# First units of a linear attention before two MLPs: products in another buffer, weight steps and key copies in another order, eight idle matmuls, later sums

## The chip, the cores and the metric

The kernel runs on one core of a Trainium2 chip as one program. The metric is the device time of one execution in microseconds (us); lower is better. The kernel before takes 982.43 us, the median of three runs (981.87 to 982.62).

## The reference

Inputs are r, k, v, w of shape (4, 8, 768, 48) (batch, heads, time, channel), u of shape (8, 48), and two pairs of MLP weights. All is float32.

```python
for t in range(S):                       # attention with a decaying state
    cur = einsum('bhd,bhe->bhde', u * kt, vt)
    y[:, :, t] = einsum('bhd,bhde->bhe', rt, state + cur)
    state = wt[..., None] * state + einsum('bhd,bhe->bhde', kt, vt)
x = y.transpose(0, 2, 1, 3).reshape(B * S, H * D)      # (3072, 384)
h = x @ moe_w_in;  x = where(h > 0, h, exp(min(h, 0)) - 1) @ moe_w_out
h = x @ moe2_w_in; x = (h / (1 + exp(-h))) @ moe2_w_out
```

Both MLPs have a hidden width of 2048.

## The kernel before

**Units.** The attention is cut into 24 units, one for each chunk of 128 steps and each batch; unit n is chunk n // 4 of batch n % 4. A unit's work has two parts. `prep_steps(n)` makes the decays: `products` (r times k, for the bonus term), `scan` and `scan_back` (the running products of w, forward and backward, in the one tile `both`), `whole_decay`, `far` (an activation over `both` that collects how small the decays get), `q` and `kt` (tiles `tq` and `tk`, scaled by the decays), `summed` (small matmuls of the products with u), and `diag` (copies the sums into `dg` and writes eight scaled identities into the tile `am`). `pe_steps(n)` holds what TensorE does and what goes with it: `scores` (tk by tq), `ktok` (a transpose of tk, tile `ktp`) and `ktok_copy` (ScalarE, into `kt`), `masked` (VectorE copies the scores over `am` above the diagonal), `outer` (kt by v, tile `upd`), `update` (VectorE, the state), `past` and `within` (the output `y`), and `split` (y into two rounded parts `xh`, ScalarE, and `xl`, VectorE).

**Weights.** An MLP's weights come in 16 pieces f0 to f15. A piece is loaded into a staging tile `wst` (three buffers), and `w_scale` (two ScalarE activations, L400 and L402), `w_join` (two VectorE operations, L409 and L411) and `w_split` (`wh` on ScalarE, L423; `wl` on VectorE, L424) make two rounded parts of it. `w_load` issues the loads of the next piece; SyncE's queue stands at that issue until the staging buffer is free.

**Stages.** `dense_units` runs the first four units alone (block 0), each turn of its loop preparing unit n + 1 while unit n is finished. Then the MLP slices begin: for each of six blocks of four units, `slot` runs 16 slices, each a `hidden` (nine matmuls, L438), an activation, and, two slices later, `out_first` (nine matmuls, L469). Between them, ticks bring the next block's units (`round_ticks`; `prep_rest` for the first of them) and, in block 0, the weight pieces. Each slice uses one weight piece. The second MLP follows.

**What sets the order.** Every engine takes its instructions in the order in which the code is written; there is no planner. What an instruction waits for are its operands and the tiles that it overwrites. Tiles of one tag go round a fixed number of buffers: `am` has two, the MLP's `gh` has two, `wst` three.

**Lines.** `products` writes at L215 and L216 into the first half of `am` (`st["af"]`), so for unit n + 1 it needs the buffer that unit n - 1 used, whose last reader is `within` (L356). The dense loop stands at L604 to L656, the ticks at L545 to L586, `prep_rest` at L658.

Of the kernel before, what the change touches and what calls it, by code (L numbers as in the profile page):

```python
# [8 lines left out]
F32 = mybir.dt.float32  # L9
# [11 lines left out]
BLOCKS = (4, 4, 4, 4, 4, 4)  # L21
# [12 lines left out]
def kernel(  # L34
# [21 lines left out]
    nc = tc.nc  # L56
# [3 lines left out]
    RB = w_ch.shape[2]  # L60
    L = 128
    NCH = S // L
    NU = B * NCH
    NP = H // 2
# [6 lines left out]
    g_p = ctx.enter_context(tc.tile_pool(name="g", bufs=2))  # L71
# [30 lines left out]
    ident = const.tile([128, 128], F32, name="ident")  # L102
# [34 lines left out]
    def load_unit(n, names):  # L137
        c, b = divmod(n, B)
        for nm in names if n < NU else "":
            if nm in "rk" and n < SUMMED:  # L140
                continue
            src, shape, pool, bufs = dict(
                w=(w_ch, [RB, W1 + 1], one_p, 2), c=(rk_ch, [RB, 2, NP, L], one_p, 2),
                r=(r_tok, [128, H * D], tok_p, 3), k=(k_tok, [128, H * D], tok_p, 3),
                v=(v_tok, [128, NP, 64 + D], tok_p, 2))[nm]
            t = un[n][nm] = pool.tile(shape, F32, tag="in_rk" if nm in "rk" else f"in_{nm}", name=f"in_{nm}", bufs=bufs)
            nc.sync.dma_start(t, src[b, c])

    def prep_steps(n):

        st = un[n]
# [60 lines left out]
        def products():  # L212
            if n >= SUMMED:
                return
            rk = st["rk"] = st["af"][0:RB, 0:NP * L].rearrange("p (j t) -> p j t", j=NP)  # L215
            nc.vector.tensor_tensor(out=rk, in0=st["c"][:, 0], in1=st["c"][:, 1], op=ALU.mult)  # L216

        def summed(p=None):
# [167 lines left out]
    def w_load():  # L386
        if not halves:
            return
        m, f = halves.pop(0)
        st = stage["st"].tile([128, 2, DM, 2], I32, tag="wst", name="wst")  # L390
        nc.sync.dma_start(st[:, 0].rearrange("p c two -> p (c two)"), (moe_w_in, moe2_w_in)[m].bitcast(I32)[f])
        src = (moe_w_out, moe2_w_out)[m].bitcast(I32)[f * 128:(f + 1) * 128, :]
        nc.sync.dma_start(st[:, 1].rearrange("p c two -> p (c two)"), src)
        loaded.append((m, f, st.rearrange("p o c two -> p (o c) two")))

    def w_scale():
        if loaded:
            m, f, st = loaded.pop(0)
            low, high = st[:, :, 0], st[:, :, 1].bitcast(F32)
            nc.scalar.activation(  # L400
                out=low, in_=low.bitcast(U32), func=ACTF.Copy, scale=(1 - 2.0**-10) * 2.0**-29, bias=-0.4927)
            nc.scalar.activation(out=high, in_=high, func=ACTF.Copy, scale=2.0**-112)  # L402
            scaled.append((m, f, st))

    def w_join():
        if scaled:
            m, f, st = scaled.pop(0)
            low, t = st[:, :, 0], st[:, :, 1]
            nc.vector.scalar_tensor_tensor(  # L409
                out=low, in0=t, scalar=-0x80000000, in1=low, op0=ALU.bitwise_and, op1=ALU.bitwise_or)  # L410
            nc.vector.scalar_tensor_tensor(  # L411
                out=t, in0=t, scalar=3, in1=low, op0=ALU.logical_shift_left, op1=ALU.bitwise_or)
            whole.append((m, f, st[:, :, 1].bitcast(F32)))

    def w_split():
        if whole:
            m, f, t = whole.pop(0)
            h = wpool.tile([128, 2, DM], F32R, tag=f"wh{f}", name=f"wh{f}_{m}")
            l = wpool.tile([128, 2, DM], F32R, tag=f"wl{f}", name=f"wl{f}_{m}")
            for i, nm in enumerate("io"):  # L420
                wh[nm, f], wl[nm, f] = h[:, i], l[:, i]
            h, l = (x.rearrange("p o c -> p (o c)") for x in (h, l))
            nc.scalar.activation(out=h, in_=t, func=ACTF.Copy)  # L423
            nc.vector.tensor_tensor(out=l, in0=t, in1=h.bitcast(F32), op=ALU.subtract)  # L424
# [106 lines left out]
    def round_parts(n, free=None):  # L531

        j = next(j for j in range(len(BLOCKS)) if n < FIRST[j + 1])
        if n == FIRST[j]:
            xts[j] = x_tile(BLOCKS[j] * L)
        pe = pe_steps(n, xts[j], (n - FIRST[j]) * L, free)
        nxt = prep_steps(n + 1) if n + 1 < NU else None

        def do(name, *a):
            if nxt:  # L540
                nxt[name](*a)

        return pe, do

    def round_ticks(n):  # L545
        pe, do = round_parts(n)

        def t0():
            pe["scores"](0)
            do("bonus")  # L550
            do("products")
            do("scan")
            load_unit(n + 2, "kr")

        def t1():
            pe["scores"](1)
            do("summed")
            do("scan_back")
            do("whole_decay")
            load_unit(n + 3, "w")  # L560
            pe["masked"](0)

        def t2():
            pe["masked"](1)
            do("far")
            do("q")
            do("diag")

        def t3():
            pe["ktok"]()  # L570
            pe["ktok_copy"]()
            do("kt")
            do("diag", 1)
            load_unit(n + 3, "c")

        def t4():
            pe["past"]()
            pe["outer"]()
            pe["update"]()

        def t5():
            pe["within"]()
            pe["split"]()
            load_unit(n + 2, "v")

        return [t0, t1, t2, t3, t4, t5]  # L586

    def dense_units():

        count = BLOCKS[0]  # L590
        prep, pe = {}, {}

        banks = [pool.tile([128, NP * L], F32, tag=tag, name="early")
                 for pool, tag, k in ((ps_o, "o", 3), (ps_h, "h", 2)) for _ in range(k)]
        sums_p = banks[2]

        def begin(n):
            pe[n], _ = round_parts(n, [banks[3 * (n % 2)], banks[3 * (n % 2) + 1]])
            pe[n]["scores"](0)
            pe[n]["scores"](1)  # L600
            pe[n]["ktok"]()
            pe[n]["ktok_copy"]()

        for n in range(-1, count):  # L604
            halves_of = iter((0, 1)) if n > 0 else ()

            def part_of_update():
                for e in islice(halves_of, 1):
                    pe[n - 1]["update"]([e])

            more = n + 1 < count
            if more:
                p = prep[n + 1] = prep_steps(n + 1)
                p["bonus"]()
                p["products"]()
                p["scan"]()
            if n == 0:
                prep[n]["diag"](0)
                prep[n]["diag"](1)
            if more:  # L620
                p["summed"](sums_p[:, (n + 1) * H:(n + 2) * H])
                p["scan_back"](part_of_update)
                p["whole_decay"]()
                p["far"]()
                p["q"]()
                p["kt"]()
                load_unit(n + 3, "wc")
            else:
                part_of_update()
                part_of_update()  # L630
            if n >= 0:
                pe[n]["masked"](0)
                pe[n]["masked"](1)
            if n > 0:
                pe[n - 1]["split"]()
            if n >= 0:
                pe[n]["outer"]()
            if more:
                begin(n + 1)
            if n >= 0:  # L640
                w_join()
                pe[n]["past"]()
                pe[n]["within"]()
                load_unit(n + 2, "v")
                if more:
                    p["diag"](0)
                    p["diag"](1)
                w_split()
                w_load()
                w_scale()  # L650
            if n == -1:
                w_start(0)
            if n == KRAT:
                nc.sync.dma_start(u_sb, u.rearrange("h d -> (h d)").unsqueeze(0).to_broadcast([128, H * D]))
        pe[count - 1]["split"]()
        pe[count - 1]["update"]()  # L656

    def prep_rest(at, p):  # L658

        if at == 1:  # L660
            p["bonus"]()
            p["products"]()
            p["scan"]()
            p["summed"]()
            p["scan_back"]()
            p["whole_decay"]()
            load_unit(BLOCKS[0] + 2, "w")
        elif at == 2:
            p["q"]()
            p["kt"]()  # L670
            load_unit(BLOCKS[0] + 2, "c")
            p["far"]()
            p["diag"](0)
            p["diag"](1)
# [302 lines left out]
```

## Time and profile before

| | us |
|---|---|
| median of three runs | 982.43 |
| profiled execution | 982.12 |
| its span | 980.3 |
| TensorE (PE) busy | 944.0 |
| VectorE (DVE) busy | 504.4 |
| ScalarE (ACT) busy | 484.7 |

The span is what the profiler saw of the engines; 1.82 us of the profiled execution lie around it. Busy times are sums over the span: they do not say which engine the others wait for in a given stretch. Times inside the trace count from the span's start. fp32 matmuls leave two records for each instruction. In brackets behind a row stands how long the engine was idle before it and which instruction ended the wait.

### The profile page before, as it was taken

The numbers are of one execution on the slowest core, as the hardware profiler recorded it, in microseconds if no ns is written. First come the engines' busy times: TensorE is split into PE (matmuls) and PEld (weight loads), VectorE is DVE, ScalarE is ACT, GpSimd is POOL, SyncE is SP. The second block draws the span as 40 slices with busy tenths as digits, with TensorE's granted clock in tenths as the row PEclk, the third lists the DMA queues.
The fourth block names the chain that finished last, engine by engine and source line by source line (L and its number), as shares of the span: only waits on it lengthen the run. The fifth ranks groups of instructions, "written<-read, shape, count | busy, mean of one in ns | idle before, by whom it ended". The sixth has DMA issues, their size and how long they took to land.

```text
span 980.3 us, 14115 instructions
## 1 busy us (share of the span) xinstructions
PE 944.0 (96%) x5622; PEld 798.5 (81%) x5622; DVE 504.4 (51%) x782; ACT 484.7 (49%) x841; POOL 134.9 (14%) x101
## 2 busy tenths in 40 slices
PE   6579999999999999999999999999999999999996
PEld 6457777788888877888778889999999999999996
DVE  6779996766766666676447874222212212212111
ACT  4568885454555554555458984333323323323322
POOL 0000003443334344433200000000000000000000
PEclk8659999999999999999999999999999999999998
DMA  8254442221221131220044550010010200200001
GB/s 243 85 166 139 163 147 67 74 80 55 89 62 55 58 103 55 80 87 10 1 145 145 167 188 1 1 65 1 33 33 1 65 1 1 65 1 1 32 1 36
DMA packets 32219, 68.63 MB, mean 70 GB/s; under 512 B 3600, under 2 KB 13968, under 8 KB 32144
## 3 DMA queue, kind: packets, MB, share of 16 engines
q1 hardware_dynamic: 32144, 67.64, 21.7%
q8 instruction: 46, 0.75, 0.3%
q14 instruction: 29, 0.24, 0.1%
HBM read 58.19 MB, written 9.44 MB: 69 GB/s over the span
## 4 chain that ended last, share of the span: by engine, by line
PE 89%; ACT 4%; DVE 3%; issue 1%; DVEq 0%; ACTq 0%
PE ph L438 40%; PE po L477 21%; PE po L469 19%; PE y L336 3%; PE sc L274 2%; PE y L356 2%; ACT am L199 1%; PE ktp L292 1%; PE upd L306 1%; ACT wh L423 1%; DVE wst L411 0%; DVE wst L409 0%; PE early L266 0%; PE sums L223 0%; ACT wst L400 0%
## 5 line engine op out<-in xcount | busy, mean ns | idle before, releaser
L461 DVE TENSOR_TENSOR gl<-g,gh 128x512 fp32r<-128x512 f32 x192 | 140.4, 731 | 312.3 <-ACT gh L460 311.9
L438 PE MATMUL ph<-xh,wh 128*128 128x512 f32 x576 | 230.7, 401 | 3.2 <-ACT xh L368 3.2
L438 PE MATMUL ph<-xl,wh 128*128 128x512 f32 x576 | 228.7, 397 | 0.0
L438 PE MATMUL ph<-xh,wl 128*128 128x512 f32 x576 | 228.0, 396 | 0.0
L460 ACT ACTIVATE gh<-g 128x512 fp32r<-128x512 f32 x192 | 120.8, 629 | 163.7 <-PE po L477 110.1
L438 PEld LDWEIGHTS ph<-xh,wh 128*128 128x128 f32 x576 | 109.6, 190 | 25.7 <-ACT xh L368 3.6
L477 PE MATMUL po<-wh,gl 128*128 128x384 f32 x384 | 129.5, 337 | 0.0
L477 PE MATMUL po<-wh,gh 128*128 128x384 f32 x384 | 129.3, 337 | 0.0
L477 PE MATMUL po<-wl,gh 128*128 128x384 f32 x384 | 129.0, 336 | 0.0
L438 PEld LDWEIGHTS ph<-xh,wl 128*128 128x128 f32 x576 | 109.5, 190 | 23.8
L438 PEld LDWEIGHTS ph<-xl,wh 128*128 128x128 f32 x576 | 109.6, 190 | 19.4 <-DVE xl L369 0.3
L449 ACT ACTIVATE g<-ph 128x512 f32<-128x512 f32 x96 | 57.3, 596 | 137.6 <-PE ph L438 137.5
L469 PE MATMUL po<-gh,wh 128*128 128x512 f32 x288 | 116.3, 404 | 0.0
L469 PE MATMUL po<-gl,wh 128*128 128x512 f32 x288 | 113.0, 392 | 0.0
L469 PE MATMUL po<-gh,wl 128*128 128x512 f32 x288 | 112.8, 392 | 0.0
L445 ACT ACTIVATE g<-ph 128x512 f32<-128x512 f32 x96 | 56.8, 592 | 89.3 <-PE ph L438 89.2
L454 DVE SCALAR_TENSOR_TENSOR g<-g,ph 128x512 f32<-128x512 f32 x96 | 65.5, 682 | 41.5 <-ACT g L447 40.7
L477 PEld LDWEIGHTS po<-wh,gh 128*128 128x128 f32 x384 | 72.2, 188 | 4.3
L477 PEld LDWEIGHTS po<-wl,gh 128*128 128x128 f32 x384 | 72.1, 188 | 4.1
L477 PEld LDWEIGHTS po<-wh,gl 128*128 128x128 f32 x384 | 72.0, 188 | 0.0
L469 PEld LDWEIGHTS po<-gh,wh 128*128 128x128 f32 x288 | 54.3, 189 | 13.0 <-issue 2.3
L227 POOL TENSOR_TENSOR ql<-tq,qh 64x512 fp32r<-64x512 f32 (+1 forms) x30 | 42.3, 1410 | 164.1 <-ACT qh L226 162.9
(88 smaller groups left out, 1108.5 us busy)
## 6 DMA issues: line engine op xcount, KB each, us to landing
wst<-in_moe_w_in_dram SPq DMA_DIRECT2D x32, 384.0 KB, 3.2
wst<-in_moe_w_out_dram SPq DMA_DIRECT2D x32, 384.0 KB, 4.1
in_c<-in_rk_ch_dram SPq DMA_DIRECT2D x24, 448.0 KB, 4.1
in_w<-in_w_ch_dram SPq DMA_DIRECT2D x24, 226.2 KB, 2.7
in_v<-in_v_tok_dram SPq DMA_DIRECT2D x24, 224.0 KB, 2.8
x_d<-x2s SPq DMA_DIRECT2D x18, 256.0 KB, 2.5
xl<-x_d SPq DMA_DIRECT2D x6, 768.0 KB, 5.2
out_dram<-os SPq DMA_DIRECT2D x24, 192.0 KB, 1.9
```

The source lines that it names most:

```text
L227: nc.gpsimd.tensor_tensor(out=lo, in0=x, in1=hi.bitcast(F32), op=ALU.subtract)
L274: nc.tensor.matmul(p[:, jj].rearrange("p e t -> p (e t)"), a[:, j, :], b[:, j].rearrange("p e t -> p (e t)"), start=i == 0, stop=i == len( ...
L336: nc.tensor.matmul(y[p0:p0 + m, kt, :], state[b][:, j, c:c + m], st["q"][:, j, :], start=kt == 0, stop=False, skip_group_check=True)
L356: nc.tensor.matmul(y[32 * base:32 * base + 32, blk // 4, :], vf[:, c:c + 32], st["a"][:, h // 2, h % 2, :], start=not ch and step == 0, st ...
L438: nc.tensor.matmul(ph, lhs, xt[rhs][:, kt, 0:nt], start=n == 0, stop=n == 3 * KT - 1)
L445: nc.scalar.activation(out=g, in_=ph, func=ACTF.Exp)
L449: nc.scalar.activation(out=g, in_=ph, func=ACTF.Silu)
L454: nc.vector.scalar_tensor_tensor(out=g, in0=g, scalar=-1.0, in1=ph, op0=ALU.mult, op1=ALU.max)
L460: nc.scalar.activation(out=gh, in_=g, func=ACTF.Copy)
L461: nc.vector.tensor_tensor(out=gl, in0=g, in1=gh.bitcast(F32), op=ALU.subtract)
L469: nc.tensor.matmul(po[ot][:, 0:nt], lhs, rhs, start=f == 0 and i == 0, stop=f == NF - 1 and i == 2)
L477: nc.tensor.matmul(po[t][:, 0:DM], lhs[:, sl], rhs["o", f], start=f == 0 and i == 0, stop=f == NF - 1 and i == 2)
```

## The change

The products of units 0 to 3 go into a buffer of the tag `gh`, which the MLP's activations use later. In the dense loop, `bonus` (which only takes the `am` buffer for these units) is called after the scans, `outer` and `begin` stand ahead of `masked`, `w_join` stands between `begin` and `masked`, and the key copy and the diagonals of unit n + 1 stand at the end of the turn, behind `w_split` and `w_scale`. After the loop there are eight matmuls of the identity with itself, whose result nobody reads; then `split` of unit 3, then the weight steps that the last turn held before. In the ticks, `summed` moves one tick later.

```diff
         def products():
             if n >= SUMMED:
                 return
-            rk = st["rk"] = st["af"][0:RB, 0:NP * L].rearrange("p (j t) -> p j t", j=NP)
+            if n < BLOCKS[0]:
+                rk = g_p.tile([RB, NP, L], F32, tag="gh", name="rk")
+            else:
+                rk = st["af"][0:RB, 0:NP * L].rearrange("p (j t) -> p j t", j=NP)
+            st["rk"] = rk
             nc.vector.tensor_tensor(out=rk, in0=st["c"][:, 0], in1=st["c"][:, 1], op=ALU.mult)
...
         def t1():
             pe["scores"](1)
-            do("summed")
             do("scan_back")
...
         def t2():
             pe["masked"](1)
+            do("summed")
             do("far")
...
             pe[n]["ktok"]()
-            pe[n]["ktok_copy"]()
+
+        def keep_clock(k):
+            for _ in range(k):
+                nc.tensor.matmul(banks[2][:, 256:384], ident, ident, start=True, stop=True)
 
         for n in range(-1, count):
...
                 p = prep[n + 1] = prep_steps(n + 1)
-                p["bonus"]()
                 p["products"]()
                 p["scan"]()
-            if n == 0:
-                prep[n]["diag"](0)
-                prep[n]["diag"](1)
-            if more:
                 p["summed"](sums_p[:, (n + 1) * H:(n + 2) * H])
                 p["scan_back"](part_of_update)
                 p["whole_decay"]()
+                p["bonus"]()
                 p["far"]()
...
             if n >= 0:
+                pe[n]["outer"]()
+            if more:
+                begin(n + 1)
+                w_join()
+            if n >= 0:
                 pe[n]["masked"](0)
                 pe[n]["masked"](1)
             if n > 0:
                 pe[n - 1]["split"]()
             if n >= 0:
-                pe[n]["outer"]()
-            if more:
-                begin(n + 1)
-            if n >= 0:
-                w_join()
                 pe[n]["past"]()
                 pe[n]["within"]()
                 load_unit(n + 2, "v")
-                if more:
-                    p["diag"](0)
-                    p["diag"](1)
+            if more:
                 w_split()
                 w_load()
-                w_scale()
+                if n >= 0:
+                    w_scale()
+                pe[n + 1]["ktok_copy"]()
+                p["diag"](0)
+                p["diag"](1)
...
+        keep_clock(8)
         pe[count - 1]["split"]()
+        w_join()
+        w_split()
+        w_load()
+        w_scale()
         pe[count - 1]["update"]()
...
             p["scan"]()
-            p["summed"]()
             p["scan_back"]()
...
         elif at == 2:
+            p["summed"]()
             p["q"]()
```

VectorE, the turn that prepares unit 2 and finishes unit 1: from `q` to the next turn's products, before.

```order
L231 TENSOR_TENSOR tq<-in_c,both 112x512
L238 TENSOR_TENSOR tk<-in_c,both 112x512
L283 COPY_PREDICATED am<-upper,early 128x4x128 x2
L369 TENSOR_TENSOR xl<-y,xh 128x3x128
L409 SCALAR_TENSOR_TENSOR wst<-wst 128x768
L411 SCALAR_TENSOR_TENSOR wst<-wst 128x768
L424 TENSOR_TENSOR wl_0_384<-wst,wh_0_383 128x768
L216 TENSOR_TENSOR am<-in_c 112x512
```

The same turn in the changed kernel, whose lines from L219 to L560 are those of before plus four.

```order
L235 TENSOR_TENSOR tq<-in_c,both 112x512
L242 TENSOR_TENSOR tk<-in_c,both 112x512
L413 SCALAR_TENSOR_TENSOR wst<-wst 128x768
L415 SCALAR_TENSOR_TENSOR wst<-wst 128x768
L287 COPY_PREDICATED am<-upper,early 128x4x128 x2
L373 TENSOR_TENSOR xl<-y,xh 128x3x128
L428 TENSOR_TENSOR wl_0_375<-wst,wh_0_374 128x768
L220 TENSOR_TENSOR rk<-in_c 112x512
```

The two joins of piece f0 moved from behind the masks to ahead of them; the products write `rk`.

ScalarE in that turn, before: from unit 2's `far` to the scaling of f1.

```order
L176 ACTIVATE am,sums<-both 112x1031
L368 ACTIVATE xh<-y 128x3x128
L298 ACTIVATE kt<-ktp 128x448
L196 ACTIVATE dg<-early 128x8
L199 ACTIVATE am<-ident,dg 128x128 x8
L423 ACTIVATE wh_0_383<-wst 128x768
L400 ACTIVATE wst<-wst 128x768
L402 ACTIVATE wst<-wst 128x768
```

And in the changed kernel.

```order
L176 ACTIVATE am,sums<-both 112x1031
L372 ACTIVATE xh<-y 128x3x128
L427 ACTIVATE wh_0_374<-wst 128x768
L404 ACTIVATE wst<-wst 128x768
L406 ACTIVATE wst<-wst 128x768
L302 ACTIVATE kt<-ktp 128x448
L196 ACTIVATE dg<-early 128x8
L199 ACTIVATE am<-ident,dg 128x128 x8
```

The weight steps moved ahead of the key copy and the diagonals.

TensorE around the third MLP slice, before: `sc` are the scores of unit 4, the sums are those of unit 5, and `ph` is the slice.

```order
L266 MATMUL sc<-tq,tk 128x128 x8
L223 MATMUL sums<-u_ch,am 128x2 x4
L438 MATMUL ph<-xh,wh_0_521 128x512
L438 MATMUL ph<-xl,wh_0_521 128x512
L438 MATMUL ph<-xh,wl_0_522 128x512
```

In the changed kernel the slice follows the scores at once, and the sums stand behind its last matmul.

```order
L442 MATMUL ph<-xh,wl_0_536 128x512
L227 MATMUL sums<-u_ch,am 128x2 x4
L473 MATMUL po<-gh,wh_0_374 128x512
```

The sums of unit 5 moved behind the nine matmuls of the third slice.

## Rows read from the trace of the kernel before

**Rows 1.** The page's part 1: busy us, share of the span, instructions.
```profile
PE 944.0 (96%) x5622; PEld 798.5 (81%) x5622; DVE 504.4 (51%) x782; ACT 484.7 (49%) x841; POOL 134.9 (14%) x101
```

**Rows 2.** Windows: length, busy us by engine, granted clock, DMA share, GB/s.
```profile
0.00:54.00 54.00, 31.22 (x337) 26.99 (x337) 36.42 (x65) 28.80 (x66) 1.74 (x9) 0.70 0.59 174
...
130.00:980.00 850.00, 842.20 (x4822) 717.38 (x4820) 398.69 (x607) 395.17 (x661) 133.18 (x92) 1.00 0.18 56
```

**Rows 3.** Timeline, VectorE, units 1 and 2: start, us, engine, line, operation.
```profile
15.27 1.36 DVE L283 COPY_PREDICATED am<-upper,early 128x512 f32<-128x512 int8 x2
19.81 0.69 DVE L216 TENSOR_TENSOR am<-in_c 112x512 f32<-112x512 f32 x1 [3.18 <-PE y L356]
...
24.61 0.68 DVE L238 TENSOR_TENSOR tk<-in_c,both 112x512 f32<-112x512 f32 x1
25.33 1.33 DVE L283 COPY_PREDICATED am<-upper,early 128x512 f32<-128x512 int8 x2
...
27.02 0.94 DVE L409 SCALAR_TENSOR_TENSOR wst<-wst 128x768 int32<-128x768 int32 x1
28.00 0.96 DVE L411 SCALAR_TENSOR_TENSOR wst<-wst 128x768 int32<-128x768 int32 x1
32.30 0.96 DVE L424 TENSOR_TENSOR wl<-wst,wh 128x768 fp32r<-128x768 f32 x1 [3.35 <-ACT wh L423]
33.18 0.68 DVE L216 TENSOR_TENSOR am<-in_c 112x512 f32<-112x512 f32 x1
```

**Rows 4.** Timeline, ScalarE, the same turn.
```profile
28.41 0.55 ACT L298 ACTIVATE kt<-ktp 128x448 f32<-128x448 f32 x1 [2.74 <-PE ktp L292]
...
29.05 2.44 ACT L199 ACTIVATE am<-ident,dg 128x128 f32<-128x128 f32 x8
31.40 0.87 ACT L423 ACTIVATE wh<-wst 128x768 fp32r<-128x768 f32 x1
32.17 0.90 ACT L400 ACTIVATE wst<-wst 128x768 int32<-128x768 uint32 x1
...
32.96 0.90 ACT L402 ACTIVATE wst<-wst 128x768 f32<-128x768 f32 x1
```

**Rows 5.** DMA issues at 10.43, 15.33 and 11.29 us: size, us to landing.
```profile
in_c<-in_rk_ch_dram SPq DMA_DIRECT2D x1, 448.0 KB, 4.6
...
in_c<-in_rk_ch_dram SPq DMA_DIRECT2D x1, 448.0 KB, 9.2
...
wst<-in_moe_w_out_dram SPq DMA_DIRECT2D x1, 384.0 KB, 5.9
```

**Rows 6.** Timeline, the last unit of the dense loop and the first slice.
```profile
46.49 0.72 DVE L320 TENSOR_TENSOR state<-upd,whole 48x192 f32<-48x192 f32 x2
...
48.10 2.53 PE L356 MATMUL y<-am,in_v 128*32 128x128 f32 x32 [4.51 <-DVE am L283]
...
53.25 0.51 ACT L368 ACTIVATE xh<-y 128x384 fp32r<-128x384 f32 x1
...
53.82 0.80 PE L438 MATMUL ph<-xh,wh 128*128 128x512 f32 x1 [3.19 <-ACT xh L368]
...
55.02 0.69 DVE L216 TENSOR_TENSOR am<-in_c 112x512 f32<-112x512 f32 x1
```

**Rows 7.** The chain that ended last: start, us, what.
```profile
53.82 4.39 PE ph L438 x9
...
67.82 1.84 PE sums L223 x8
...
130.01 2.27 PE ph L438 x9
```

**Rows 8.** TensorE's waits, 54 to 140 us: total, times, longest.
```profile
PE sums L223 <- DVE seed L156: 4.8, 3, 3.3
```

**Rows 9.** Timeline: the third slice's exponential on ScalarE.
```profile
73.58 0.60 ACT L445 ACTIVATE g<-ph 128x512 f32<-128x512 f32 x1 [1.28 <-PE ph L438]
```

**Rows 10.** Windows over the 16 warm-up matmuls alone: TensorE busy (records).
```profile
1.10:4.90 3.80, 3.80 (x18) 3.80 (x19) 1.00 0.80 225
```

## The prediction

> **What bounds the kernel now.** I read the busy times first, then the stages, the timeline of the dense loop, and the chain that ended last. TensorE is busy for 944.0 of 980.3 us [rows 1], and from 130 us on for 842.20 of 850 us [rows 2]: there it sets the time, and nothing of the change lies there. In the first 54 us it is busy for 31.22 us only [rows 2]. So a microsecond won ahead of the MLP moves all that follows, as long as the slices up to 130 us do not give it back.
>
> In the first 54 us the loop of a turn sets the time. VectorE makes `tk` (ends 24.61 + 0.68 = 25.29), TensorE scores and transposes it, ScalarE copies the keys at 28.41, writes the diagonals until 31.49 and only then `wh` at 31.40 to 32.27 [rows 4]. VectorE meanwhile masks and joins, stands idle for 3.35 us for `wh`, writes `wl` at 32.30 and begins the next unit at 33.18 [rows 3]. A turn is 33.18 - 19.81 = 13.37 us [rows 3]; the next one is 46.49 - 33.18 = 13.31 us [rows 3, 6]. Ahead of that, VectorE waits 3.18 us at 19.81 for `within` of unit 0, because the products overwrite its `am` [rows 3].
>
> **The change part by part.** I follow VectorE.
>
> Products in a `gh` buffer: the wait of 3.18 us goes. What is late next is VectorE itself, which ends the masks at 15.27 + 1.36 = 16.63 [rows 3], and unit 2's r and k, which land at 10.43 + 4.6 = 15.03 [rows 5]. Unit 2 starts at 16.63 instead of 19.81: -3.2 us. The MLP's own first use of these buffers comes after the first slice, so that the ring costs nothing.
>
> Joins ahead of the masks, weight steps ahead of the key copy: `wh` no longer stands behind the diagonals on ScalarE. VectorE's turn becomes products to `tk` 25.29 - 19.81 = 5.48 us, a step of 0.04, the joins 28.96 - 27.02 = 1.94, masks and `xl` 27.02 - 25.33 = 1.69, `wl` to the next products 33.18 - 32.30 = 0.88 [rows 3], together 10.03 us. `wh` (0.87 us [rows 4]) runs beside the masks and `xl`, which take longer, so the 3.35 us go. Unit 3 starts at 26.66 instead of 33.18, -6.5 us, and the state update of the last turn at 36.69 instead of 46.49 [rows 6], -9.8 us. Three covers are needed. Unit 3's r and k land at 15.33 + 9.2 = 24.53 [rows 5], 2.1 us ahead of their use; what issues them comes before 16.63 and does not move. The scaling of f0 moves ahead of unit 1's key copy and now waits for its bytes, 11.29 + 5.9 = 17.19 [rows 5]; two activations of 0.9 later it is 19.0, and the key copy is late by some 0.2 us, beside unit 2's scans. And the diagonals of unit 2 come 2.46 us later on ScalarE (31.40 to 33.86, `wh` and two scalings [rows 4]), but VectorE asks for them a whole preparation later. SyncE's queue keeps its order; the load that stands there until `wl` of f0 is done, with unit 3's v and unit 4's inputs behind it, goes with that `wl`, 6.5 us earlier.
>
> The last turn has no preparation, and there the order on ScalarE shows: the joins of f1 end at 26.66 + 5.52 + 1.94 = 34.12, then `wh` and scalings 2.46, then key copy to the last diagonal 31.49 - 28.41 = 3.08 [rows 4]: 39.7. VectorE would mask at 36.69 + 0.72 = 37.4 and waits 2.3 us, a new wait. Before, the masks began at 46.49 + 0.72 = 47.21 [rows 6]; the gain falls to -7.5 us. `within` of unit 3 then runs 40.6 to 43.1 instead of 48.10 to 50.63.
>
> The first slice: before, it stood 3.19 us after `within`, since ScalarE did weight work ahead of `xh` [rows 6]. Now `xh` comes first, and the slice could start 53.82 - 53.25 = 0.57 us after `within`. But the eight idle matmuls stand ahead of it on TensorE. Matmuls of this very shape (128 by 128 fp32) left 18 records in 3.80 us [rows 10], 0.21 each; 16 records are 3.4 us at that pace and half of it, 1.7, at the full clock. So the slice starts at 46.5 (44.8): -7.3 (-9.0) us. I take -7.3, the end that goes by the row's own pace.
>
> The first slice takes 4.39 us before, against 2.27 for nine such matmuls later [rows 7], a ratio near that of the clock's two levels. Now TensorE has run without a gap since 40.6. The saving lies between 0 and 2.1 us; I take 1.5. The exponential behind it starts at 49.4 instead of 58.2: -8.8 us.
>
> Sums later: unit 5's sums stood ahead of the third slice and waited 3.3 us for VectorE [rows 8], then ran 1.84 [rows 7], and ScalarE idled 1.28 us for that slice [rows 9]. Now the slice does not wait. ScalarE's chain gets between 0 and 1.3 us, TensorE up to 5.1; I take ScalarE's 1.3, since ScalarE and VectorE are behind with the weight pieces there. -10.1 us. Two more such waits, 4.8 - 3.3 = 1.5 us [rows 8], go wholly or not at all: 0.8. Sum: -10.9 us.
>
> The profiled execution took 982.12, 0.3 below the median. 982.12 - 10.9 = 971.2; with the 0.3 half counted, 971.3.
>
> One rule speaks against it. TensorE's rows say 31.22 of 54 us busy in the stage that changes, 842.20 of 850 in the last one [rows 2]. The Trainium skill, "Perfetto Trace Analysis", section "Identifying the Most-Contended Engine", says to find the engine with the highest occupancy and work on that first. Taken over the whole span that is TensorE, to which the change only adds; by the rule the sum would be +1.7 to +3.4 us. The same page grants that a kernel can have several regimes, and the rows show two.
>
> **The rivals.**
> - *The gain of the dense loop, and no more* (975.6). The weight steps of f2 now come after `xl` of unit 3. On VectorE: `xl` ends near 44.2, joins 1.94, `wh` 0.8, `wl` 0.9, the update 0.7: unit 4's products at 48.5 instead of 55.02 [rows 6], -6.5 us. If VectorE's string of decays and weight pieces sets the pace up to 130 us, that is all that arrives: 982.1 - 6.5. For it: two engines share that work and TensorE waited for products three times there [rows 8]. Against: the last of those waits are what the sums' move takes away.
> - *More* (967.5). Full clock for the idle matmuls (-1.7), the whole 2.1 us of the first slice and 1.5 us of the sums: -10.9 - 1.7 - 0.6 - 0.7 = -13.9 gives 968.2, and TensorE's 5.1 us at the third slice may add a little.
> - *The new buffer frees nothing* (974.5): `far` still writes `am`. Were VectorE held by that as before, the 3.2 us would stay. Against: `far` is on ScalarE, and the next scan alone asks for it.
> - *No change*: unit 3's inputs come so late that the loop falls back to its old times. They would have to land 6.5 us + 2.1 later than now; their issue does not move.
> - *Slower* (984 to 985). TensorE takes its work in order, and the idle matmuls delay the first slice by up to 3.4 - 0.57 = 2.8 us. If TensorE's own order sets the end from the first slice on and the loop gives less than 2.8 us, the result is a loss of up to 2.8 us. It decides at a loop gain of 2.8; for it speaks TensorE's share of 96% [rows 1], against it 22.8 idle us in the first 54 [rows 2]. It is the case of the skill's rule above.
>
> **How the numbers follow.** The forecast with 968.5 to 973.5 gets 0.64; the dense loop's gain alone 0.18; more 0.08; the buffer that frees nothing 0.04; no change 0.03; slower 0.03. About 0.2% (2 us) is what a measurement of this kernel can tell from no change. Faster by more than that: 0.94; within: 0.03; slower: 0.03. The range goes from 967.5 (half of "more") to 976.5 (the dense loop's case and an error of 0.9 in its sum).
>
> **What the profile of the changed kernel would show.** The products of unit 2 at 16.6 with no wait for `y`; units 3 and the last update near 26.7 and 36.7; a new wait of 2 us of the last masks for the diagonals; `wh` without 3.35 us idle on VectorE behind it. The first slice near 46.5, most of it at the 2.4 GHz level. The third slice directly behind the scores, and no 3.3 us wait of the sums. Wrong would be: unit 3's products waiting for a DMA; VectorE waiting for ScalarE in the turns of units 1 and 2; a first slice later than 48; or a gain at 130 us that is over 2 us smaller than at the first slice.

## The result and the profile after

The changed kernel takes 970.12 us (median, 969.58 to 971.15) against 982.15 us for the kernel before in the same runs: ratio 0.988, 95% interval 0.9863 to 0.9897. The forecast was 971.3 us.

The page's part 1 of the changed kernel, beside [rows 1]: the engines do the same work. TensorE's 1.1 us more are the idle matmuls (3.59 us), less what ran at a higher clock (2.0 us at the first slice alone).

```profile
span 968.2 us, 14152 instructions
...
PE 945.1 (98%) x5638; PEld 798.5 (82%) x5638; DVE 504.2 (52%) x782; ACT 485.0 (50%) x841; POOL 135.0 (14%) x101
```

Windows of the changed kernel, columns as in [rows 2]. In the first 54 us VectorE is now busy for 43.16 us (36.42 before) and ScalarE for 34.27 (28.80). Between 54 and 130 us VectorE is the fullest engine, 73.01 of 76 us (69.30 before, in the same window), ahead of TensorE's 71.12. Behind 130 us TensorE is as full as it was.

```profile
0.00:54.00 54.00, 43.21 (x378) 36.55 (x378) 43.16 (x77) 34.27 (x77) 1.74 (x9) 0.68 0.65 197
54.00:130.00 76.00, 71.12 (x506) 53.74 (x508) 73.01 (x117) 63.94 (x120) 0.00 (x0) 0.98 0.49 158
130.00:960.00 830.00, 829.46 (x4750) 707.22 (x4751) 387.16 (x588) 385.66 (x644) 133.27 (x92) 1.00 0.17 54
```

VectorE's timeline through the dense loop and to unit 5's products, to be read against [rows 3] and [rows 6].

```profile
5.21 0.69 DVE L220 TENSOR_TENSOR rk<-in_c 112x512 f32<-112x512 f32 x1 [3.65 <-DMA in_c<-in_rk_ch_dram]
...
15.16 1.34 DVE L287 COPY_PREDICATED am<-upper,early 128x512 f32<-128x512 int8 x2
16.40 0.67 DVE L220 TENSOR_TENSOR rk<-in_c 112x512 f32<-112x512 f32 x1
...
25.48 0.94 DVE L428 TENSOR_TENSOR wl<-wst,wh 128x768 fp32r<-128x768 f32 x1
26.34 0.68 DVE L220 TENSOR_TENSOR rk<-in_c 112x512 f32<-112x512 f32 x1
...
36.23 0.72 DVE L324 TENSOR_TENSOR state<-upd,whole 48x192 f32<-48x192 f32 x2
38.92 1.33 DVE L287 COPY_PREDICATED am<-upper,early 128x512 f32<-128x512 int8 x2 [1.96 <-ACT am L199]
...
42.80 0.56 DVE L373 TENSOR_TENSOR xl<-y,xh 128x384 fp32r<-128x384 f32 x1 [2.11 <-ACT xh L372]
...
46.18 0.96 DVE L428 TENSOR_TENSOR wl<-wst,wh 128x768 fp32r<-128x768 f32 x1 [0.96 <-ACT wh L427]
...
47.80 0.69 DVE L220 TENSOR_TENSOR am<-in_c 112x512 f32<-112x512 f32 x1
...
57.56 0.68 DVE L220 TENSOR_TENSOR am<-in_c 112x512 f32<-112x512 f32 x1
```

Of the kernel before, the first products of unit 0 and those of unit 5:

```profile
5.48 0.69 DVE L216 TENSOR_TENSOR am<-in_c 112x512 f32<-112x512 f32 x1 [3.92 <-DMA in_c<-in_rk_ch_dram]
...
67.00 0.68 DVE L216 TENSOR_TENSOR am<-in_c 112x512 f32<-112x512 f32 x1
```

The products of unit 2 follow the masks at 16.40 and wait for nothing; `wl` follows `xl` without the 3.35 us of before. The new wait is that of the last masks for the diagonals, 1.96 us (2.3 was forecast); behind it the last `xl` waits 2.11 us for `xh`, where it waited 1.02 before. This execution's first products start at 5.21 us; before they started at 5.48. So 0.27 us of each difference of positions is the start and not the change.

TensorE's and ScalarE's timelines from the last unit to the third slice, with TensorE's last matmul.

```profile
39.70 2.53 PE L360 MATMUL y<-am,in_v 128*32 128x128 f32 x32 [1.44 <-DVE am L287]
42.16 3.59 PE L609 MATMUL early<-ident 128*128 128x128 f32 x16
45.51 0.48 PE L442 MATMUL ph<-xh,wh 128*128 128x512 f32 x1
...
57.31 0.79 PE L442 MATMUL ph<-xh,wh 128*128 128x512 f32 x1
...
960.97 0.34 PE L481 MATMUL po<-wh,gl 128*128 128x384 f32 x1
```
```profile
47.88 0.60 ACT L449 ACTIVATE g<-ph 128x512 f32<-128x512 f32 x1
...
51.56 1.07 ACT L176 ACTIVATE am<-both 112x1031 bf16<-112x1031 f32 x1 [0.84 <-DVE whole L181]
...
62.74 0.59 ACT L449 ACTIVATE g<-ph 128x512 f32<-128x512 f32 x1
```

Before, the first slice's exponential and the last matmul:

```profile
58.23 0.60 ACT L445 ACTIVATE g<-ph 128x512 f32<-128x512 f32 x1 [4.46 <-PE ph L438]
```
```profile
971.86 0.34 PE L477 MATMUL po<-wh,gl 128*128 128x384 f32 x1
```

Windows of the changed kernel over the idle matmuls and over the first slice, columns as in [rows 2]:

```profile
42.16:45.75 3.59, 3.59 (x19) 3.59 (x18) 2.38 (x3) 0.99 (x2) 0.00 (x0) 0.55 0.78 199
45.51:47.84 2.33, 2.33 (x12) 1.58 (x10) 1.62 (x4) 2.23 (x3) 0.00 (x0) 1.00 0.04 12
```

The eight idle matmuls take 3.59 us, most of it at the 1.2 GHz level (granted clock 0.55). The first slice starts at 45.51 (53.82 before [rows 6]) and runs at the 2.4 GHz level (1.00), and its exponential comes at 47.88, not at 58.23: -10.35 us. The third slice's comes at 62.74 against 73.58 [rows 9]: -10.84 us. From there on nothing changes: the last matmul starts at 971.86 before and at 960.97 after, -10.89 us.

TensorE's waits from 44 to 130 us, beside [rows 8]: waited for what, total, times, longest.

```profile
PE sc L270 <- DVE tk L242: 3.6, 1, 3.6
...
PE sums L227 <- DVE seed L156: 0.8, 1, 0.8
```

The chain that ended last, 42 to 62 us, answers to [rows 7]. Before, it went through the first slice. Now, up to 57 us, it goes through VectorE and ScalarE alone: `xl`, the joins, `wh`, the state, unit 4's products and scans, its `far` and diagonals, and `wh` and `wl` again. Behind that it has the load of a weight piece, beside which VectorE goes on without a wait.

```profile
42.80 0.04 DVE xl L373
...
47.80 0.69 DVE am L220
...
51.56 1.16 ACT am L176 x2
...
55.26 0.80 ACT wh L427
...
57.07 2.40 DMA wst<-in_moe_w_in_dram
```

The profiled executions differ by 982.12 - 970.0 = 12.1 us: 0.27 at the start, 10.89 - 0.27 = 10.62 up to the last matmul, and 1.2 behind it, for which the forecast had nothing. The last instruction of VectorE before and then of the changed kernel:

```profile
972.60 0.36 DVE L504 COPY os<-po 128x192 f32<-128x192 f32 x1 [0.85 <-ACT os L502]
```
```profile
961.71 0.36 DVE L508 COPY os<-po 128x192 f32<-128x192 f32 x1 [0.85 <-ACT os L506]
```

From its end to the end of the span are 980.3 - 972.96 = 7.3 us before and 968.2 - 962.07 = 6.1 us after.

### The profile page after: what moved, and what is told of

It reads as the page before. It is cut to its first block, busy times and chain, and to the rows that moved or that the text cites. A ratio compares the mean times of both kernels' runs of the same rounds, so it can differ in the third digit from the quotient of the medians.

```text
span 968.2 us, 14152 instructions
## 1 busy us (share of the span) xinstructions
PE 945.1 (98%) x5638; PEld 798.5 (82%) x5638; DVE 504.2 (52%) x782; ACT 485.0 (50%) x841; POOL 135.0 (14%) x101
## 4 chain that ended last, share of the span: by engine, by line
PE 86%; DVE 5%; ACT 4%; issue 1%; DMA 1%; SPq 0%; DVEq 0%
PE ph L442 39%; PE po L481 21%; PE po L473 18%; PE y L340 3%; PE sc L278 2%; PE y L360 2%; ACT am L199 1%; DVE wst L413 1%; DVE wst L415 1%; ACT wh L427 1%; PE upd L310 1%; DMA in_v<-in_v_tok_dram 1%; DVE wl L428 1%; DVE both L157 1%; DVE gl L465 0%
## 5 line engine op out<-in xcount | busy, mean ns | idle before, releaser
L442 PE MATMUL ph<-xl,wh 128*128 128x512 f32 x576 | 226.4, 393 | 0.0
```

What stands on the lines that cost most here:

```text
L442: nc.tensor.matmul(ph, lhs, xt[rhs][:, kt, 0:nt], start=n == 0, stop=n == 3 * KT - 1)
```

## The experiments

Each ran beside the kernel before, whose median was 982.72 us with the first four variants, 982.87 with the next four, 982.93 with the two after them and 982.52 with the last; beside the changed kernel it was 982.15. The same kernel's medians so lie up to 0.8 us apart, and a smaller difference between the medians of two variants says little. The traces say more: behind the experiments stands a table that counts from unit 2's products.

**The buffer alone.** The kernel before with the products in a `gh` buffer.

```diff
-            rk = st["rk"] = st["af"][0:RB, 0:NP * L].rearrange("p (j t) -> p j t", j=NP)
+            if n < BLOCKS[0]:
+                rk = g_p.tile([RB, NP, L], F32, tag="gh", name="rk")
...
```

> The kernel before with one edit: the products of units 0 to 3 go into a gh buffer; all orders stay as before. Theory (a turn's wait goes and the rest of the loop keeps its length): VectorE's products of unit 2 begin near 16.5 us instead of 19.8 with no wait for y, everything behind moves by 3.2 us, 979.0 us. Rival (the wait returns elsewhere in the loop, at the diagonals or the inputs): 981.5 to 982.2.

Measured: 977.21 us, ratio 0.9948 (0.9934 to 0.9961). In its trace unit 2's products start at 17.54 us and wait for nothing.

**The order alone**, the changed kernel with products and `bonus` back in `am`:

```diff
-            if n < BLOCKS[0]:
-                rk = g_p.tile([RB, NP, L], F32, tag="gh", name="rk")
...
+                p["bonus"]()
                 p["products"]()
```

> The changed kernel with the products of units 0 to 3 back in the am buffer (bonus ahead of them again); orders, idle matmuls and later sums as changed. Theory (parts add up): VectorE waits near 3 us for y of unit 0 ahead of unit 2's products; in the changed kernel y of unit 1 ends at 27.9, so unit 3's products wait too, from 26.3 + 3.2 on not much; 970.1 + 3.2 = 973.3 us. Rival (the new order leaves slack that covers the wait): 970.1 to 971.

Measured: 974.98 us, 0.9927 (0.9913 to 0.9941). VectorE's timeline of this variant:

```profile
19.62 0.69 DVE L216 TENSOR_TENSOR am<-in_c 112x512 f32<-112x512 f32 x1 [3.41 <-PE y L356]
...
30.93 0.69 DVE L216 TENSOR_TENSOR am<-in_c 112x512 f32<-112x512 f32 x1 [1.28 <-PE y L356]
```

Both miss their theory's number, by 1.8 and 1.7 us, but on the side away from the rival's: the buffer and the order each give a part. In the second, the two waits for `y`, 3.41 and 1.28 us, are what is lost: from the first products to the last matmul it takes 960.43 us, the changed kernel 955.76, 4.67 less. The theory had the second of them at near nothing. In the first, the tail behind the last matmul is 1.5 us shorter than before (1.2 in the second), which is most of the miss. Without the tails the gains are 5.5 - 1.5 = 4.0 and 7.7 - 1.2 = 6.5 us, together 10.5; the whole change, beside its own runs of the kernel before, gains 12.0 - 1.2 = 10.8. The parts add up as far as these medians can tell.

**Without the idle matmuls.**

```diff
-        keep_clock(8)
```

> The changed kernel without the eight idle matmuls. Theory A (the string of decays and weight pieces on VectorE and ScalarE sets the time up to 131 us, so the first slice's clock is hidden): the first slice starts near 42.8 instead of 45.5 at the low clock, takes near 3.5 to 4.4 us, and the end stays, 970.1 within 0.7 us. Theory B (as predicted: the clock of the first slice is worth 1.5 us to what follows): 971.6 us or more. Theory C (the idle matmuls only delay): 967.3 us.

Measured: 969.52 us, 0.987 (0.9855 to 0.9885). The eight matmuls make no difference that these intervals can tell: without them the first slice starts earlier in its trace (43.80) but runs at the lower level, granted clock 0.50:

```profile
43.80:47.90 4.10, 4.10 (x9) 2.79 (x9) 3.09 (x4) 1.67 (x3) 0.00 (x0) 0.50 0.47 109
```

**Sums early again.**

```diff
             pe["scores"](1)
+            do("summed")
             do("scan_back")
...
             pe["masked"](1)
-            do("summed")
             do("far")
...
             p["scan"]()
+            p["summed"]()
             p["scan_back"]()
...
         elif at == 2:
-            p["summed"]()
             p["q"]()
```

> The changed kernel with the sums back at the earlier tick. As predicted (the move is worth 1.3 us on ScalarE's chain at the third slice and 0.8 us at two later waits): the third slice waits again for the sums, its exponential comes 1.3 us later, 972.2 us. Rival (VectorE and ScalarE set the pace up to 131 us, TensorE's waits are slack): 970.1 to 970.8 us.

Measured: 972.2 us, 0.9894 (0.9879 to 0.9909). TensorE's waits in this variant, 44 to 130 us, and the third slice's exponential:

```profile
PE sums L227 <- DVE seed L156: 3.4, 4, 1.3
```
```profile
65.32 0.60 ACT L449 ACTIVATE g<-ph 128x512 f32<-128x512 f32 x1 [1.47 <-PE ph L442]
```

The median is the theory's number to the tenth, but the parts are not the theory's. Counted from unit 2's products (17.41 us here, 16.40 in the changed kernel), the exponential is 1.57 us later and the last matmul 1.61: the sums cost 1.6 us at the third slice, where 1.3 were forecast, and the two later waits next to nothing, where 0.8 were. The profiled execution is 0.9 us later still, because unit 0's scores ran at the lower clock in it, which comes up again below. The rival, by which TensorE's waits are slack, falls.

**The end of the kernel.** The kernel before with 24 one-column fills on VectorE in the second MLP.

```diff
+                if j == 2 and f < 8:
+                    for c in range(3):
+                        nc.vector.memset(near[:, 2 + c:3 + c], 1.0)
```

> The kernel before, plus 24 one-column fills on VectorE in the second MLP, three behind a down-projection of each of eight slices; they write columns that nothing reads. Theory A: in the kernel before, the last step of VectorE stands 2.5 us behind its last instruction because a piece of its instruction stream is fetched there, and another number of instructions moves that fetch away from the end. Then the tail behind the last matmul falls from 8.35 us to about 7.0, as in all four variants so far, the last matmul stays where it was, and the time is 981.2 us (980.9 to 981.7). Theory B: the gap belongs to the end of this program and not to the count of instructions; the fills are hidden beside TensorE and the time is that of before (982.4 to 982.8). Theory C: the fills cost on the path, 24 times about 0.06 us at most: 983 to 984.

Measured: 981.51 us, 0.9988 (0.9979 to 0.9997): more instructions, 1.4 us less, over executions that spread from 980.0 to 982.74. The last matmul did not stay where it was: in the profiled execution it starts at 972.73, 0.87 us later than before, because `within` of unit 0 ran at the lower clock (1.94 us instead of 1.08) and unit 2's products waited for it. The tail is what the theory said. In this trace VectorE's last copy ends at 973.83, 5.9 us ahead of the span's end of 979.7. The instruction packets of one of the DMA queues, from VectorE's last copy to the end of the span, before, in this variant and in the changed kernel:

```profile
q14 instruction: 7, 0.06, 2.4%
```
```profile
q14 instruction: 6, 0.05, 2.7%
```
```profile
q14 instruction: 6, 0.05, 2.7%
```

In all three, packets of instructions land when all computing is done. Before has one more than the others, 0.2 us ahead of the end and 2.5 us behind the one before it; the last of this variant comes 1.3 us ahead of the end, that of the changed kernel 1.8. That fits theory A for the tail. It is not shown that the end waits for that packet, nor whose instructions it holds; that fills on VectorE alone go with its absence is what speaks for VectorE. And there is one trace of the kernel before.

**Last turn: scaling behind the diagonals.**

```diff
-                if n >= 0:
+                if 0 <= n < 2:
                     w_scale()
                 pe[n + 1]["ktok_copy"]()
                 p["diag"](0)
                 p["diag"](1)
+                if n == 2:
+                    w_scale()
```

> The changed kernel with one step of unit 3's turn moved: its key copy and its diagonals now come ahead of the scaling of weight pieces on ScalarE, so the masks of unit 3 do not wait for the diagonals behind that scaling (they waited 1.96 us). Theory A (the string of VectorE and ScalarE steps through unit 3 to the products of units 4 and 5 sets the end of the first MLP's start, TensorE does not): the masks come up to 1.9 us earlier, what is late next is the join of the third slice's weights, which now waits for the later scaling; the third slice's exp comes 0.5 to 1.9 us earlier and the time is 969.0 us (968.3 to 969.7). Theory B (the scaling is needed just as early by the join, so that the wait only changes its place): 970.0 to 970.6. Theory C (the join is late by more than the masks gain, and the products of unit 4 behind it): 971 to 972.

Measured: 969.33 us, 0.986 (0.9845 to 0.9875). VectorE's timeline of this variant:

```profile
37.94 1.35 DVE L287 COPY_PREDICATED am<-upper,early 128x512 f32<-128x512 int8 x2 [0.77 <-ACT am L199]
...
46.83 0.69 DVE L220 TENSOR_TENSOR am<-in_c 112x512 f32<-112x512 f32 x1
```

The masks wait 0.77 us, not 1.96; unit 4's products come 0.97 us earlier, and so does the third slice's exponential. Theory A holds.

**Join ahead of the split.**

```diff
-        pe[count - 1]["split"]()
         w_join()
+        pe[count - 1]["split"]()
```

> The changed kernel with the join of the third slice's weights ahead of the split of unit 3's heads instead of behind it. Theory A (the same VectorE string sets the time, and the join waited 0.96 us at its place only for ScalarE): order of the two does not change their sum, and the time is 970.1 us within 0.5. Theory B: the third slice's weights are what its first matmul waits for; joined earlier they let it start up to 1 us earlier: 969.1 to 969.5. Theory C: the split is what the first slice waits for, and its later end delays it by the length of the join: 971 or more.

Measured: 969.71 us, 0.9866 (0.9851 to 0.9882), inside theory A's range, but the trace is against A. `xl` waits 0.26 us instead of 2.11, since the joins now fill that wait. Counted from unit 2's products, unit 4's come 2.6 us earlier, the first slice and its exponential no earlier, and the last matmul 0.8 us earlier. So the order does count, and not by the way of theory B, which had the first slice start sooner.

**Both moves, and TensorE kept busy ahead of unit 0's scores.** Both edits above, and:

```diff
+                if n == -1:
+                    keep_clock(9)
                 p["scan_back"](part_of_update)
...
-        keep_clock(8)
```

> The changed kernel with both moves (unit 3's key copy and diagonals ahead of the scaling of weights; the third slice's join ahead of the split), without the idle matmuls ahead of the first slice, and with nine idle matmuls instead behind unit 0's first sums, so that TensorE is not idle ahead of unit 0's scores. Theory A: in the profiled executions of three of the four variants so far unit 0's scores ran at the lower clock (2.08 us for what took 1.16), and its masks then waited 1.05 us for the diagonals; with TensorE busy ahead of them they run at the higher clock in every execution, and with what the two moves give, the time is 968.0 us (967.2 to 969.0). Theory B: the clock at unit 0 is hidden by what units 1 and 2 wait for anyway; only the two moves count: 969.0 to 969.7. Theory C: the nine idle matmuls stand in front of unit 0's work on TensorE and delay it by up to their own length (about 2 us): 971 to 972.

Measured: 967.54 us, 0.9843 (0.9829 to 0.9856), the fastest of all.

**Both moves alone**, without the nine matmuls (and without the eight):

> The changed kernel with both moves (unit 3's key copy and diagonals ahead of the scaling of weights; the third slice's join ahead of the split) and without the idle matmuls ahead of the first slice, but with none behind unit 0's first sums: the variant that took 967.54 us, without its nine idle matmuls. Theory A: the moves alone give what was gained there, and the clock at unit 0 costs only in those executions in which it has fallen by 10 us, about 1 us in three of four of the profiles of changed kernels that were alike in this: 968.0 to 968.6 us. Theory B: the clock at unit 0 counts for nothing in the time, and it is that variant's 967.5 within 0.3. Theory C: the moves count for little, and the nine idle matmuls gave the 2 us: 969.2 us or more.

Measured: 968.64 us, 0.9855 (0.9841 to 0.9868), 0.04 us above theory A's range.

**The nine matmuls alone**, added to the changed kernel:

> The changed kernel with its eight idle matmuls ahead of the first slice, and nine more behind unit 0's first sums; nothing is moved. Theory A: it takes away a cost of about 1 us in those executions in which TensorE's clock has fallen ahead of unit 0's scores: 969.4 to 969.9 us, and unit 0's scores run at the higher clock in its profile, with no wait of its masks for the diagonals above 0.2 us. Theory B: nothing changes at the end (970.0 to 970.3). Theory C: the nine cost the 2 us that the moves have won in the other variant: 971 or more.

Measured: 969.82 us, 0.9871 (0.9856 to 0.9886). The scores and masks of unit 0 in the timelines of TensorE and VectorE, first with the moves alone, then with the nine matmuls alone:

```profile
10.32 2.08 PE L270 MATMUL early<-tq,tk 64*128 64x128 f32 x16 [2.22 <-DVE tk L242]
...
16.22 1.35 DVE L287 COPY_PREDICATED am<-upper,early 128x512 f32<-128x512 int8 x2 [1.06 <-ACT am L199]
```
```profile
10.26 1.16 PE L270 MATMUL early<-tq,tk 64*128 64x128 f32 x16 [0.74 <-DVE tk L242]
...
15.01 1.33 DVE L287 COPY_PREDICATED am<-upper,early 128x512 f32<-128x512 int8 x2
```

Windows over those scores, in the one and in the other, columns as in [rows 2]:

```profile
10.32:12.40 2.08, 2.08 (x17) 1.85 (x18) 1.95 (x4) 0.00 (x0) 0.00 (x0) 0.50 0.75 199
```
```profile
10.26:11.42 1.16, 1.16 (x17) 1.04 (x18) 1.06 (x3) 0.00 (x0) 0.00 (x0) 1.00 0.63 175
```

The granted clock is 0.50, the 1.2 GHz level, in the one and 1.00, the 2.4 GHz level, in the other. Behind a 2.22 us gap the scores of unit 0 take 2.08 us, kept busy 1.16, and the 1.06 us wait of the masks goes. It is 1.1 us with the two moves (968.64 to 967.54): in the traces 1.2 us from the first products to unit 2's, and nothing behind them. Without the moves the medians differ by 0.3 (970.12 to 969.82), which is less than they can tell, and the traces by 0.2: an execution in which the clock has not fallen by then, as in the profiled one of the changed kernel, has nothing to win. The moves alone give 970.12 - 968.64 = 1.5 us by the medians.

**Three times the idle matmuls.**

```diff
-        keep_clock(8)
+        keep_clock(24)
```

> The changed kernel with 24 idle matmuls ahead of the first slice instead of eight. The 16 more run at the pace that the clock then grants, 3.6 us at the higher level (7.2 at the lower), and the first slice and its exponential come later by as much. Theory A: between the first exponential and unit 4's collecting activation on ScalarE (which waited 0.84 us for VectorE) there is a slack of about 0.9 us, and behind it the delay passes on whole: 970.1 + 3.6 - 0.9 = 972.8 us (972.3 to 973.5). Theory B: the first slice sets the end, with no slack: 973.7 or more. Theory C: VectorE's weight pieces and decays set the end up to 120 us and take in all of it, as they took in the eight: 969.6 to 970.6.

Measured: 973.58 us, 0.9908 (0.9892 to 0.9925), 3.5 us over the changed kernel. TensorE's timeline of this variant, windows over its idle matmuls, and ScalarE's timeline:

```profile
42.99 7.50 PE L609 MATMUL early<-ident 128*128 128x128 f32 x48
```
```profile
42.99:46.60 3.61, 3.61 (x19) 3.61 (x18) 2.38 (x3) 1.01 (x2) 0.00 (x0) 0.50 0.83 201
46.60:50.20 3.60, 3.60 (x32) 3.60 (x32) 3.11 (x6) 1.98 (x3) 0.00 (x0) 0.95 0.27 74
```
```profile
52.61 0.60 ACT L449 ACTIVATE g<-ph 128x512 f32<-128x512 f32 x1 [4.03 <-PE ph L442]
...
55.38 1.06 ACT L176 ACTIVATE am<-both 112x1031 bf16<-112x1031 f32 x1
```

Counted from the first products, the exponential is 4.81 us later than in the changed kernel (3.91 of it the sixteen matmuls, 0.9 a late unit 0) and the last matmul 3.92: 0.9 us are taken in, and `far` stands right behind ScalarE's work of the first slice, without the 0.84 us wait. That is theory A's slack in the trace; the median lies 0.1 us above A's range and 0.1 below B's number, and would not have settled it alone.

**All traces, counted from the products.** In microseconds, from the starts in each profiled execution: unit 0's scores (their length), from the first products to those of unit 2, and from those to the last matmul.

| | scores of unit 0 | to unit 2's products | from there to the last matmul |
|---|---|---|---|
| the changed kernel | 1.16 | 11.19 | 944.57 |
| without the idle matmuls | 2.08 | 12.11 | 944.66 |
| sums early again | 2.08 | 12.10 | 946.18 |
| scaling behind the diagonals | 1.26 | 11.28 | 943.44 |
| join ahead of the split | 2.08 | 12.11 | 943.77 |
| both moves alone | 2.08 | 12.12 | 942.34 |
| both moves, nine matmuls | 1.16 | 10.95 | 942.33 |
| the nine matmuls alone | 1.16 | 10.97 | 944.57 |
| 24 idle matmuls | 2.08 | 12.11 | 947.57 |

The first two columns hold the clock at unit 0, the last one the edits behind it: nothing for the eight idle matmuls, 1.6 us for the later sums, 1.1 and 0.8 for the two moves, 2.2 for both, 3.0 lost by sixteen more idle matmuls. Both moves were run only without the eight idle matmuls, so their 2.2 us is with these gone; what the moves give with them is not shown.

## Why the prediction was right, point by point

- *The buffer* (-3.2 us): the products of unit 2 came 3.4 us earlier, 3.1 without the start. `far` held nobody up, so the rival of a buffer that frees nothing falls.
- *The dense loop* (-6.5, then -9.8): -6.6 and -10.0 without the start. Joins, key copy, diagonals and `outer` moved together in every run, so what each gives alone is not shown. All three covers held: no load made VectorE wait in the loop, and ScalarE waited 0.16 us for the bytes of f0.
- *The new wait of the last masks* (2.3 us): 1.96, and unit 3's masks at 38.92 against 39.7.
- *The first slice* (-7.3, exponential -8.8): -8.3 and -10.35. `within` ended 0.9 us earlier than forecast (0.27 of it the start), and the slice got the full clock, 2.0 us saved where 1.5 was taken.
- *The step that failed in its route, not in its sum*: the exponential's gain was passed on whole to what follows. It is not. Unit 4's products came only -7.2 us (55.02 to 47.80), near the -6.5 of the rival "the gain of the dense loop". Before, ScalarE had that exponential and its weight scaling in front of unit 4's `far`, and VectorE then waited for `wh` (2.99 us, now 0.77); now they are done 0.84 us before VectorE has the scans ready. Unit 5's products so come at 57.56 instead of 67.00 (before, in the same timeline), -9.4 us, of which 2.2 were won between the two. With the 1.4 us of the sums that is -10.8. The string of decays and weight pieces on VectorE and ScalarE sets the end of this stage, as that rival said, and VectorE is busy for 73.01 of its 76 us; but its pace was not fixed, because an early first slice takes work out of ScalarE's way.
- *The idle matmuls*: 3.4 us of delay were forecast, and 45.51 - 42.23 = 3.3 came. The sum is near, its reading was not: the row that it goes by shows a granted clock of 1.00 [rows 10], so 0.21 us for a record was not the lower level's pace by that row, and half of it not the full clock's. The paces come from the run with 24: at a granted clock of 0.50 it left 19 records in 3.61 us, at 0.95 then 32 in 3.60 us. Why the warm-up was slow at 1.00 is not shown. The clock gave back 2.0 us at the first slice. What is left of the delay, less the 0.57 that the slice would have waited for `xh`, is 0.7 us and falls into the slack of 0.9; without them the time is the same, and sixteen more cost 3.5 us. That was the mechanism of the rival "slower": it decides from the slack on, and eight stay below it.
- *The later sums* (1.3 + 0.8): on the path the third slice gained 1.4, and the two later waits 0.05 (-10.84 to -10.89), not 0.8. Undone alone they cost 1.6 us in the trace; that the medians differ by the 2.1 of the forecast is chance.
- *Missing*: the 1.2 us at the end of the kernel. Up to the last matmul 10.9 us were forecast and 10.6 measured (10.9 with the start); that the median lies 1.2 us under the forecast is nearly all the tail.

That the sum came so near is in part luck. Without the start, the exponential of the first slice gained 10.1 us where 8.8 were forecast, 0.9 was lost on the way to unit 5's products where nothing was, the sums gave 1.4 for 1.3, and the later waits 0.05 for 0.8: errors that cancel to 0.3 us. The mechanism up to the first slice, the waits that go and the one that comes, is as forecast.

The Trainium skill's rule on the engine with the highest occupancy ("Perfetto Trace Analysis", section "Identifying the Most-Contended Engine") taken over the whole span names TensorE, and by it the change, which only adds to TensorE, had nothing to win. The runs decide against that: TensorE got more work, and the time fell by 12 us. In the first 54 us, where the change lies, the busiest engine was VectorE, 36.42 us against TensorE's 31.22 [rows 2]; taken by stage, the rule names the engine whose waits went.

## What to carry to other kernels

When two engines share a string of small work in front of a full one, follow the orders of both turn by turn, and ask at each gain how much of it the next engine can use: 10.35 us at the first slice were 9.4 us at the next unit, and the 0.9 between them is what the idle matmuls could use up for nothing. An instruction that must come early belongs ahead of one that has a turn's time, and the last turn has to be checked alone, since nothing follows in it that would cover a wait: there two moves were still worth 1.5 us by the medians and 2.2 in the traces. When executions of one kernel take two courses, count from a point behind the fork before the medians are compared.

## What was not expected of the hardware

- The tail behind the last copy depends on more than the work in it: 7.3 us from VectorE's last copy to the end of the span before, 5.9 with 24 fills added in the middle, and 1.4 us less in the median; in the traces of all twelve other programs run here it is 5.8 to 6.4 us. A late packet of instructions is the likely cause, not a shown one. A difference of that size between two kernels says nothing on the step that was changed, if the last matmul does not show it. The Trainium skill, "Runtime: NRT & Kernel Launch", section "Instruction fetch mechanics", calls the cost of going from one block of instructions to the next mostly hidden; the one packet that lands 0.2 us ahead of the end before may be a case where it was not.
- The same code has two courses at unit 0. In some executions the granted clock has fallen to the lower level, behind a gap of some 2 us, when unit 0's scores start; they then take 2.08 us instead of 1.16, and all that follows is about 1 us later. The gap alone does not decide it: behind 2.22 us the scores ran at 0.50 with the moves alone, behind 2.47 us at 0.97 in the changed kernel. Nine matmuls without use in the gap made the kernel faster by 1.1 us with the two moves.
